# Attention, feed-forward and gMLP on one core: one-bank accumulators in phase two, and earlier buffers for group 0's sums

## The chip, the cores and the metric

The kernel runs on one core of a Trainium2 chip. Every product is made on TensorE (PE) and summed in PSUM, whose eight banks hold 128 x 512 f32 numbers each. VectorE (DVE), ScalarE (ACT) and GpSimd (POOL) take the sums out and prepare operands; SyncE (SP) issues the DMAs. The metric is the device time of one execution in microseconds (us).

## The reference

For 8 batches of 576 positions and a width of 512, three stages follow each other:

```python
out  = softmax(q_c @ k_c.T / 8) @ v_c           # 8 heads, chunks of 64 positions
x    = x + relu(LN(x) * g @ w_ch1) @ w_ch2      # 512 -> 2048 -> 512
h    = gelu_tanh(x @ w_in)                      # 512 -> 1024
u, v = h[..., :512], h[..., 512:]
v_s  = w_sg @ (LN(v) * g_ln) + b_sg             # over the 576 positions
out  = x + (u * v_s) @ w_out
```

The x of the second line is the attention's output, its heads side by side.

## The kernel before, in words

**Numbers.** A product of f32 matrices is made from fp16 halves: each operand is split into a rounded half ("hi") and the rest ("lo"), and three matmuls (hi·hi, hi·lo, lo·hi) are summed. Most large products also use seven products of quarter blocks in place of eight. Such a product needs sums and differences of quarters ahead of it (three instructions on DVE), a rounding to hi (ACT) and a subtraction for lo (DVE or POOL).

**Phase one.** The 8 x 576 positions are 36 tiles of 128, in 18 blocks of two. A block goes through attention, the layer norm, ff1 and ff2. For blocks 4 to 17 this is done in eight passes: `ff1p(b, j)` makes 24 matmuls (L639), ACT takes the result through relu (L654), DVE makes the sums (L661 to L663), ACT rounds (L666) and DVE or POOL subtracts (L668); `ff2p(b, j)` then makes 21 matmuls (L690), two passes later. After the last pass of a block DVE (L708), ACT (L713) and POOL (L718) put its x together, a DMA stores it in `x2d` in DRAM (L574), and DVE takes its largest magnitude (L201). In the middle of phase one the weights of phase two are split too, through buffers of the pool `stB`, which `close_st` closes when that is done.

**Group 0's x2 sums.** Phase two works on four groups of 9 tiles. For each group x is loaded again, as five panels p = 0 to 4 (`x2_make`): loads into `xs` (L900), sums on DVE (L907 to L909, panels 0 to 3), rounding on ACT into `hh` (L924), subtraction on DVE (L927), and two DMA transpositions, of the hi and of the lo half, into `x2T` (L922). For group 0 this is part of phase one's plan (`first_x2`). It has one `xs` and one `hh` buffer, allocated in the pool `x2L`, which `open_x2` opens where the attention's pool has been closed, thus after the attention of block 17. Its lo half goes into a buffer of the ring `xT`, which is the operand of ff1p.

**Phase two.** Each group makes v (L1206, L1231), u (L1248, L1269), the spatial product in two halves e = 0 and 1 (`s_units`: four units each, one 128 x 512 matmul L1301 and one 128 x 64 matmul L1302 per step; evacuated on DVE by L1312 and, for the 64-wide part, L1331; multiplied by u on POOL, L1319), the scale of the gated product (`red` by DVE, transposed on PE by L206), its halves, and nine `o_unit`s (product L1381, evacuated with the addition of x by L1389 on DVE). The outputs of v and u are taken out by ACT (L1113) and DVE (L1117).

**What sets the order.** The class `Plan` holds every operation with its engine, an assumed duration, a priority and the keys that it reads and writes. It plays the program through with the assumed durations and writes the instructions in the order that results; phase one is one plan, phase two another. Waits between instructions are put in by the framework, per tile: an instruction that writes a tile waits for the earlier readers of that tile.

**PSUM.** One pool, `psA`, is open throughout. It has two tiles of two banks, `pair0` and `pair1`, and four of one, `bank2`, `bank3`, `bank6` and `bank7`. Phase two takes accumulators from a ring `R` of eight one-bank pieces by `take`, so that four of the pieces are halves of a pair:

```python
R = [bank[2], bank[3], pair[1][:, 0], pair[1][:, 1], pair[0][:, 0], pair[0][:, 1], bank[6], bank[7]]
```

Of the kernel before, what the change touches and what calls it, by code (L numbers as in the profile page):

```python
# [9 lines left out]
F16 = mybir.dt.float16  # L10
F32 = mybir.dt.float32
# [121 lines left out]
def fused_kernel(ctx: ExitStack, tc, qkv, w1, w2, g1, w_in, w_out, wsgt, wsgs, g2, b_sg, out):  # L133
# [4 lines left out]
    small = ctx.enter_context(tc.tile_pool(name="small", bufs=1))  # L138
    dram = ctx.enter_context(tc.tile_pool(name="dram", bufs=1, space=bass.MemoryType.DRAM))
    psA = tc.tile_pool(name="psA", bufs=1, space=PSUM)  # L140
    ps = ctx.enter_context(psA)
    pair = [ps.tile([P, 2, 512], F32, name=f"pair{i}") for i in range(2)]
    bank = {i: ps.tile([P, 512], F32, name=f"bank{i}") for i in (2, 3, 6, 7)}
    x2d = [dram.tile([P, D], F32, name=f"x2d{t}") for t in range(NT)]
# [15 lines left out]
    def close_pool(key):  # L160
        pools.pop(key)[0].__exit__(None, None, None)
# [692 lines left out]

    def close_st():
        bW["stp"].__exit__(None, None, None)

    def open_x2():
        close_pool("att")
        p = ctx.enter_context(tc.tile_pool(name="x2L", bufs=1))  # L860
        x2p["T"] = p.tile([P, 2, 7, 2, D], F16, name="x2T")
        x2p["T8"] = p.tile([P, 2, 4, P], F16, name="x2T8")
        x2p["xs"] = [p.tile([P, 9, 256], F32, name="xs0")]
        x2p["hh"] = [p.tile([P, 7 * 256], F16, name="hh0")]

    def x2_cols(g0, n):

# [16 lines left out]
    def x2_make(pl, g, p, pr):  # L884


        o = pl.op
        xs, X = x2_buf(pl, "xs")
        hi, H = x2_buf(pl, "hh")
        if pl is plan:  # L890
            lo = x2p.get("lo") or palloc("xT", 2, [P, 2, 4, 256], F16, px)
            x2p["lo"], L = lo, lambda: lo.t.rearrange("p a k t -> p (a k t)")
        else:
            lo, L = x2_buf(pl, "hh")
        if p < 4:
            tiles, a, n = ((g * GT + p + 4, (0, 2)), (g * GT + p, (1, 3))), 1, 7
        else:
            tiles, a, n = ((g * GT + 8, (0, 1)),), 0, 2
        for t, c in tiles:
            o("SP", 730, lambda t=t, c=c: nc.sync.dma_start(  # L900
                out=X()[:, c[0]:c[1] + 1:c[1] - c[0]], in_=x2d[t].rearrange("p (n e) -> p n e", n=2)
            ), rd=["x2L"] + [f"x2d{t}"] * (pl is plan), wr=[xs], lat=2200, prio=pr)

        def sums():
            a = X()
            two = lambda x, y: a[:, x:y + 1:y - x]
            nc.vector.tensor_tensor(out=two(6, 8), in0=two(1, 3), in1=two(0, 2), op=ALU.subtract)  # L907
            nc.vector.tensor_tensor(out=two(4, 7), in0=two(0, 6), in1=two(2, 8), op=ALU.add)
            nc.vector.tensor_tensor(out=a[:, 5], in0=a[:, 2], in1=a[:, 6], op=ALU.subtract)  # L909

        if p < 4:
            o("DVE", 1800, sums, wr=[xs], prio=pr)
        src = lambda: X()[:, a:a + n].rearrange("p n e -> p (n e)")
        w = n * 256
        sc = i2g[:, g:g + 1]

        def turned(x, b, B):
            if p < 4:
                out, c = x2p["T"][:, x].rearrange("p n k t -> p (n k) t"), slice(p * 128, p * 128 + 128)
            else:  # L920
                out, c = x2p["T8"][:, x], slice(0, 128)
            nc.sync.dma_start_transpose(out=out[:, :, c], in_=B()[:, 0:w])  # L922

        o("ACT", 60 + w, lambda: nc.scalar.activation(out=H()[:, 0:w], in_=src(), func=AF.Copy, scale=sc),  # L924
          rd=[xs, f"sx{min(g, 1)}"], wr=[hi], prio=pr)

        o("DVE", 80 + w * 26 // 25, lambda: nc.vector.scalar_tensor_tensor(  # L927
            out=L()[:, 0:w], in0=src(), scalar=sc, in1=H()[:, 0:w], op0=ALU.mult, op1=ALU.subtract
        ), rd=[xs, f"sx{min(g, 1)}", hi], wr=[lo], prio=pr)

        def last():
            for x, b, B in ((0, hi, H), (1, lo, L)):
                o("SP", 1300 * n // 4, lambda x=x, b=b, B=B: turned(x, b, B), rd=[b], wr=[f"xT{x}{p}"], lat=2200, prio=pr)

        return last

    def first_x2():
        pr = 9500
        op("DVE", 100, lambda: absmax(redg[:, 0:1], x2mx[:, 0:GT]), rd=[f"x2mx{i}" for i in range(GT)], wr=["redg"], prio=pr)
        par(e2g[:, 0:1], redg[:, 0:1], ["redg"], ["x2e"], pr)  # L940
        op("DVE", 600, lambda: x2_cols(0, 1), rd=["win_s"], wr=["x2e", "sx0"], prio=pr)
        for p in range(5):
            x2_make(plan, 0, p, pr)()

    tops = [Buf(f"top{i}", None) for i in range(2)]
    with tc.manual_schedule():
# [76 lines left out]
        for b in range(B0, NB):  # L1023
# [7 lines left out]
            if b in (B0 + 1, B0 + 2, B0 + 3):  # L1031
                half[b - B0 - 1]()
            if b == B0 + 3:
                op(None, 0, close_st, rd=["wsg_s"] + done, wr=["Braw", "Btmp", "topB", "stC"], prio=0)
        for b, j in todo:
            ff2p(b, j)
        op(None, 0, open_x2, rd=["stC"], wr=["x2L"] + ATT, prio=0)
        first_x2()
        nff.append(0)

# [6 lines left out]
        plan.idle = busy  # L1047
        plan.run()

        close_pool("w2s")  # L1050
        pX.__exit__(None, None, None)
        wA.__exit__(None, None, None)
# [13 lines left out]

        plan2 = Plan()
        op2 = plan2.op
        R = [bank[2], bank[3], pair[1][:, 0], pair[1][:, 1], pair[0][:, 0], pair[0][:, 1], bank[6], bank[7]]
        turn_, seq = [0], [0]  # L1070
        xk = [f"xT{x}{p}" for x in range(2) for p in range(5)]
        op2(None, 0, lambda: None, wr=xk + ["x2L", "sx0", "ident"])

        def take(n):
            r = [(turn_[0] + k) % 8 for k in range(n)]
# [427 lines left out]
```

## Time and profile before

| | |
|---|---|
| median of 3 runs | 1282.22 us (1281.65 to 1283.42) |
| the profiled execution's own time | 1283.95 us |
| its span | 1282.2 us |
| TensorE busy | 1210.5 us, 94% |
| VectorE busy | 819.9 us, 64% |
| ScalarE busy | 558.8 us, 44% |
| GpSimd busy | 485.2 us, 38% |
| mean granted clock of TensorE | 0.991 |
| phase one's last product ends at | 865.8 us |

Times in rows are microseconds from the start of the span. Names of tiles stand without their numbers, so that `pair` is either of the two pairs, and `bank` any of the four single banks. A granted clock of 1 is 2.4 GHz, and 0.5 is 1.2 GHz. In a bracket behind a row stands the idle time of the engine before it, and what ended it.

### The profile page before, as it was taken

How to read it: one execution, taken by the hardware profiler on the slowest of the kernel's cores; microseconds unless marked ns; L12 is line 12 of the kernel's file. 1: busy time of each engine (PE TensorE's matmuls, PEld its weight loads, DVE VectorE, ACT ScalarE, POOL GpSimd, SP SyncE). 2: the span in 40 equal slices, each digit the busy share in tenths (PEclk: the TensorE clock that was granted, in tenths of full speed). 3: DMA queues.
4: the chain of work that ended last, by engine and by line, in shares of the span. 5: the costliest groups of instructions: out<-in, count | busy, mean ns of one | idle time of the engine just before them, and what ended most of it. 6: DMA issues, size and time to landing. Idle time of an engine off the chain costs nothing. (4 is left out here: it accounts for less than half of the span.)

```text
span 1282.2 us, 27034 instructions
## 1 busy us (share of the span) xinstructions
PE 1210.5 (94%) x11412; PEld 893.1 (70%) x11412; DVE 819.9 (64%) x1520; ACT 558.8 (44%) x844; POOL 485.2 (38%) x415
## 2 busy tenths in 40 slices
PE   7899999898998999999999999988899999999998
PEld 5687644677887888888888888866455556446453
DVE  6885135988677656665665565666778378457445
ACT  6776303455764533334333333333544444434320
POOL 3553203544585644434444334422432131232220
PEclk9999999999999999999999999999999999999999
DMA  9762002274222222122122201443353462362203
GB/s 319 242 210 80 1 33 75 75 208 127 83 59 59 59 67 67 51 67 65 55 64 57 69 26 50 92 99 91 85 129 107 86 153 91 86 121 66 82 1 115
DMA packets 140377, 117.81 MB, mean 92 GB/s; under 512 B 104928, under 2 KB 113120, under 8 KB 140256
## 3 DMA queue, kind: packets, MB, share of 16 engines
q1 hardware_dynamic: 140256, 116.09, 33.3%
q8 instruction: 89, 1.46, 0.5%
q14 instruction: 32, 0.26, 0.1%
HBM read 72.02 MB, written 18.87 MB: 71 GB/s over the span
## 5 line engine op out<-in xcount | busy, mean ns | idle before, releaser
L639 PE MATMUL bank<-xT,w1h 128*128 128x256 f16 x1792 | 304.1, 274 | 0.4 <-DVE x L568 0.4
L690 PEld LDWEIGHTS <-arena 128*128 128x128 f16 x2352 | 229.4, 99 | 44.5 <-issue 8.0
L639 PE MATMUL bank<-xT,w1l 128*128 128x256 f16 x896 | 245.6, 274 | 0.0
L668 POOL TENSOR_TENSOR arena<-arena 128x896 f16<-128x896 f32 x69 | 132.5, 1920 | 223.8 <-ACT arena L666 223.7
L639 PEld LDWEIGHTS <-w1h 128*128 128x128 f16 x1792 | 173.9, 98 | 23.5 <-issue 1.2
L666 ACT ACTIVATE arena<-arena 128x896 f16<-128x896 f32 x112 | 106.2, 949 | 186.4 <-DVE arena L663 102.2
L661 DVE TENSOR_TENSOR arena<-arena 128x256 f32<-128x256 f32 x112 | 76.2, 681 | 103.4 <-ACT arena L654 103.2
L690 PE MATMUL pair<-w,arena 128*128 128x256 f16 x672 | 112.3, 276 | 6.2 <-ACT arena L666 4.3
L690 PE MATMUL pair<-w2s,arena 128*128 128x256 f16 x672 | 111.5, 275 | 5.7 <-ACT u L713 5.2
L654 ACT ACTIVATE arena<-bank 128x512 f32<-128x512 f32 x112 | 66.4, 593 | 108.2 <-PE bank L639 108.2
L1319 POOL TENSOR_TENSOR uT<-uT,vs 128x512 f32<-128x512 f32 x30 | 47.1, 1571 | 135.9 <-DVE vs L1312 105.6
L639 PEld LDWEIGHTS <-w1l 128*128 128x128 f16 x896 | 88.2, 98 | 10.7
L690 PE MATMUL bank<-w,arena 128*128 128x256 f16 x672 | 93.2, 275 | 0.0
L535 PE MATMUL bank<-xT,w1h 128*128 128x256 f16 x512 | 86.9, 274 | 3.8 <-DMA xT<-hl 2.7
L718 POOL TENSOR_TENSOR x<-x,u 128x256 f32<-128x256 f32 (+1 forms) x60 | 65.2, 1116 | 45.9 <-DVE x L708 34.1
L1206 PEld LDWEIGHTS <-x2T 128*128 128x128 f16 x672 | 66.2, 99 | 17.7 <-issue 7.4
L1381 PE MATMUL pair<-wout,gh 128*128 128x512 f16 x208 | 61.9, 379 | 8.9 <-DVE xr L1389 7.0
L535 PE MATMUL bank<-xT,w1l 128*128 128x256 f16 x256 | 70.2, 274 | 0.0
L668 DVE TENSOR_TENSOR arena<-arena 128x896 f16<-128x896 f32 x43 | 57.5, 1337 | 19.7 <-ACT arena L666 19.7
L1301 PE MATMUL pair<-wsg,vh 128*128 128x512 f16 x190 | 60.1, 380 | 9.0 <-DVE vs L1312 8.1
L535 PEld LDWEIGHTS <-w1h 128*128 128x128 f16 x512 | 49.2, 98 | 15.1 <-issue 3.1
L662 DVE TENSOR_TENSOR arena<-arena 128x256 f32<-128x256 f32 x112 | 54.7, 488 | 3.8
(274 smaller groups left out, 2381.3 us busy)
## 6 DMA issues: line engine op xcount, KB each, us to landing
straw<-in_w SPq DMA_DIRECT2D x16, 1023.8 KB, 6.0
qkl<-in_qkv SPq DMA_DIRECT2D x26, 512.0 KB, 3.7
x2d<-x SPq DMA_DIRECT2D x36, 256.0 KB, 2.0
xs<-x2d SPq DMA_DIRECT2D x36, 256.0 KB, 3.3
xr<-x2d SPq DMA_DIRECT2D x36, 256.0 KB, 2.9
out<-xr SPq DMA_DIRECT2D x36, 256.0 KB, 2.5
vl<-in_qkv SPq DMA_DIRECT2D x26, 256.0 KB, 2.7
qk<-in_qkv SPq DMA_DIRECT2D x10, 512.0 KB, 6.1
```

Source lines behind the costliest of these rows:

```text
L535: nc.tensor.matmul(acc, lhsT=w[j][:, k, fc], rhs=xT.t[:, x, k], start=(n == 0), stop=(n == 11))
L639: nc.tensor.matmul(acc[:, y * 256:y * 256 + 256], lhsT=w[j][:, k, fc], rhs=xT.t[:, x, k], start=(n == 0), stop=(n == 11),)
L654: op("ACT", 600, lambda: nc.scalar.activation(out=o.t[:, 0:4].rearrange("p n t -> p (n t)"), in_=acc, func=AF.Relu, scale=0.5), rd=[kb] + ...
L661: nc.vector.tensor_tensor(out=two(6, 8), in0=two(1, 3), in1=two(0, 2), op=ALU.subtract)
L662: nc.vector.tensor_tensor(out=two(4, 7), in0=two(0, 6), in1=two(2, 8), op=ALU.add)
L666: op("ACT", 950, lambda: nc.scalar.activation(out=h.t[:, 0], in_=o.t[:, 1:8], func=AF.Copy), rd=[o] + ar, wr=[h], prio=-100)
L668: op(lo[0], lo[1], lambda: lo[2].tensor_tensor(out=h.t[:, 1], in0=o.t[:, 1:8], in1=h.t[:, 0], op=ALU.subtract), rd=[o], wr=[h], prio=-100)
L690: nc.tensor.matmul(acc, lhsT=h.t[:, x, n], rhs=r(y), start=(first and j == 0 and m == 0), stop=(j == 7 and m == 2), skip_group_check=True,)
L718: op("POOL", ns, lambda: nc.gpsimd.tensor_tensor(out=d(), in0=d(), in1=v(), op=ALU.add), rd=u + ["q6", "q5", "q7"], wr=[x], prio=-50)
L1206: nc.tensor.matmul(ap[:, q * 256:q * 256 + 256], lhsT=xT[:, x, a, k, c], rhs=right(b, 1, k, w), start=(first and n == 0), stop=(k == 1 and ...
L1301: nc.tensor.matmul(ap, lhsT=v[:, fc], rhs=w[:, 0:512], start=(n == 0), stop=end)
L1381: nc.tensor.matmul(ap, lhsT=x[:, k, c], rhs=w[:, k], start=(n == 0), stop=(n == 11))
```

## The change

It has two parts. First, `psA` is closed after phase one's plan, and a pool `psB` of eight tiles of one bank each, `pb0` to `pb7`, is opened. The ring `R` lists them in the order 4, 5, 2, 3, 0, 1, 6, 7, which are the same banks in the same places as before. Second, `xs0` and `hh0` are allocated in a new pool `xsL` in the room of `stB`, when `close_st` runs. The loads of group 0 now need that pool alone, and the transpositions need `x2L`. The hi half is transposed first; for panels 0 and 1 the lo half then overwrites `hh0`, and for panels 2 to 4 it goes into the `xT` buffer as before. Line numbers from L857 on are 3 to 9 higher after the change, and 9 higher in phase two: L907 to L909 are L910 to L912, L927 is L936, L1206 is L1215, L1301 is L1310, L1381 is L1390.

```diff
-    ps = ctx.enter_context(psA)
+    ps = psA.__enter__()
...
     def close_st():
         bW["stp"].__exit__(None, None, None)
+        p = ctx.enter_context(tc.tile_pool(name="xsL", bufs=1))
+        x2p["xs"] = [p.tile([P, 9, 256], F32, name="xs0")]
+        x2p["hh"] = [p.tile([P, 7 * 256], F16, name="hh0")]
...
     def open_x2():
...
-        x2p["xs"] = [p.tile([P, 9, 256], F32, name="xs0")]
-        x2p["hh"] = [p.tile([P, 7 * 256], F16, name="hh0")]
...
     def x2_make(pl, g, p, pr):
...
-        if pl is plan:
+        if pl is not plan:
+            lo, L = x2_buf(pl, "hh")
+        elif p < 2:
+            lo, L = hi, H
+        else:
             lo = x2p.get("lo") or palloc("xT", 2, [P, 2, 4, 256], F16, px)
             x2p["lo"], L = lo, lambda: lo.t.rearrange("p a k t -> p (a k t)")
-        else:
-            lo, L = x2_buf(pl, "hh")
...
-            ), rd=["x2L"] + [f"x2d{t}"] * (pl is plan), wr=[xs], lat=2200, prio=pr)
+            ), rd=["xsL"] + [f"x2d{t}"] * (pl is plan), wr=[xs], lat=2200, prio=pr)
...
+        def turns(*xs_):
+            for x, b, B in xs_:
+                o("SP", 1300 * n // 4, lambda x=x, b=b, B=B: turned(x, b, B), rd=["x2L", b], wr=[f"xT{x}{p}"], lat=2200, prio=pr)
+
+        if pl is plan:
+            turns((0, hi, H))
         o("DVE", 80 + w * 26 // 25, lambda: nc.vector.scalar_tensor_tensor(
             out=L()[:, 0:w], in0=src(), scalar=sc, in1=H()[:, 0:w], op0=ALU.mult, op1=ALU.subtract
-        ), rd=[xs, f"sx{min(g, 1)}", hi], wr=[lo], prio=pr)
+        ), rd=[xs, f"sx{min(g, 1)}"] + [hi] * (hi is not lo), wr=[lo], prio=pr)
+        if pl is plan:
+            return turns((1, lo, L))
+        return lambda: turns((0, hi, H), (1, lo, L))
...
         plan.run()
 
+        psA.__exit__(None, None, None)
+        psB = ctx.enter_context(tc.tile_pool(name="psB", bufs=1, space=PSUM))
+        bank = [psB.tile([P, 512], F32, name=f"pb{i}") for i in range(8)]
...
-        R = [bank[2], bank[3], pair[1][:, 0], pair[1][:, 1], pair[0][:, 0], pair[0][:, 1], bank[6], bank[7]]
+        R = [bank[k] for k in (4, 5, 2, 3, 0, 1, 6, 7)]
```

On TensorE, in group 0's spatial product, the start of the second half of a unit's matmuls. `pair1_64` and `pb3` are the same bank there, `vh` and `vl` the halves of v, `wsg` those of w_sg. Before:

```order
L1301 LDWEIGHTS vh_10698
L1301 MATMUL pair1_64<-wsg_3164,vh_10698 128x512 [waits DVE_49]
L1302 LDWEIGHTS vh_10698
L1302 MATMUL bank3_66<-wsg_3164,vh_10698 128x64
L1301 LDWEIGHTS vl_10699
```

The same rows after the change:

```order
L1310 LDWEIGHTS vh_10713
L1310 MATMUL pb3_10695<-wsg_3164,vh_10713 128x512
L1311 LDWEIGHTS vh_10713
L1311 MATMUL pb5_10697<-wsg_3164,vh_10713 128x64
L1310 LDWEIGHTS vl_10714
```

The wait for DVE is gone in this row; in all, 18 matmuls of L1301 and 17 of L1381 have a wait for another engine in the order before, and 11 and 7 after. No row of phase two has another place on any engine.

On TensorE, at the border of the phases: the last matmuls of phase one (`w2s7` and `arena` are the operands of its last ff2p pass) and the first of phase two. Before:

```order
L690 LDWEIGHTS arena_114
L690 MATMUL bank7_68<-w2s7_2552,arena_114 128x256
L1206 LDWEIGHTS x2T_9921 [waits DMAHW4_49,PE_49]
L1206 MATMUL bank2_65<-win_3162,x2T_9921 128x256
L1206 LDWEIGHTS x2T_9921
```

After:

```order
L690 LDWEIGHTS arena_114
L690 MATMUL bank7_68<-w2s7_2552,arena_114 128x256
L1215 LDWEIGHTS x2T_9932 [waits DVE_49,DMAHW4_49,PE_49]
L1215 MATMUL pb4_10696<-win_3162,x2T_9932 128x256 [waits Activation_49]
L1215 LDWEIGHTS x2T_9932
```

The first product now waits for DVE and ScalarE too: for the last L708 and the last L713, which read tiles of the old pool.

On DVE, at the end of phase one, the rows up to the last ff2 evacuation (L661 to L663 are an ff1p pass's sums, L668 its subtraction, `xs0` group 0's panel). Before, panel 3:

```order
L907 TENSOR_TENSOR xs0_9923<-xs0_9923 128x2x256 [waits DMAHW1_49,DMAHW0_49]
L908 TENSOR_TENSOR xs0_9923<-xs0_9923 128x2x256 [waits DVE_49]
L909 TENSOR_TENSOR xs0_9923<-xs0_9923 128x256
L927 SCALAR_TENSOR_TENSOR xT_10140<-xs0_9923,i2g_128,hh0_9924 128x1792 [waits DMAHW7_49,Activation_49]
L661 TENSOR_TENSOR arena_114<-arena_114 128x2x128 [waits Activation_49]
L662 TENSOR_TENSOR arena_114<-arena_114 128x2x128 [waits DVE_49]
L663 TENSOR_TENSOR arena_114<-arena_114 128x128
L668 TENSOR_TENSOR arena_114<-arena_114 128x896 [waits PE_49,Activation_49]
L708 SCALAR_TENSOR_TENSOR x_10651<-pair0_63,c_c2b_175,x_10651 128x256 [waits PE_49,Activation_49]
```

After, from panel 3's subtraction on:

```order
L936 SCALAR_TENSOR_TENSOR xT_10330<-xs0_5485,i2g_128,hh0_5486 128x1792 [waits DMAHW6_49,Activation_49]
L661 TENSOR_TENSOR arena_114<-arena_114 128x2x128 [waits Activation_49]
L662 TENSOR_TENSOR arena_114<-arena_114 128x2x128 [waits DVE_49]
L663 TENSOR_TENSOR arena_114<-arena_114 128x128
L668 TENSOR_TENSOR arena_114<-arena_114 128x896 [waits PE_49,Activation_49]
L661 TENSOR_TENSOR arena_114<-arena_114 128x2x128 [waits Activation_49]
L662 TENSOR_TENSOR arena_114<-arena_114 128x2x128 [waits DVE_49]
L663 TENSOR_TENSOR arena_114<-arena_114 128x128
L936 SCALAR_TENSOR_TENSOR xT_10330<-xs0_5485,i2g_128,hh0_5486 128x512 [waits DMAHW4_49,DMAHW3_49,Activation_49]
L661 TENSOR_TENSOR arena_114<-arena_114 128x2x128 [waits Activation_49]
L662 TENSOR_TENSOR arena_114<-arena_114 128x2x128 [waits DVE_49]
L663 TENSOR_TENSOR arena_114<-arena_114 128x128
```

Before, panel 3's sums and subtraction stand directly ahead of the last pass's sums, and panel 4's subtraction (128x512) behind the last L708; after, two other passes' sums stand between panel 3's subtraction and the last pass's, and panel 4's subtraction is ahead of the last pass's. Panel 0's sums stand where block 8 is worked on, some 400 DVE rows before its subtraction, and its two loads on SP ahead of a load of q and k. The subtractions of panels 0 and 1 have one wait, for a DMA (the transposition of `hh0`). On TensorE two small pieces of phase one have another place: a group of the attention's transpositions (L304) comes three matmuls later, and at the border of blocks 16 and 17 an ff2p pass that was split around half an ff1p pass is whole.

## Rows read from the trace of the kernel before

**Rows 1.** The page, part 1: busy us, share of the span, instructions.

```profile
PE 1210.5 (94%) x11412; PEld 893.1 (70%) x11412; DVE 819.9 (64%) x1520; ACT 558.8 (44%) x844; POOL 485.2 (38%) x415
```

**Rows 2.** TensorE's waits: line, what ended them: us in total, times, longest.

```profile
PE pair L1301 <- DVE vs L1312: 8.1, 9, 1.3
PE pair L1381 <- DVE xr L1389: 7.0, 8, 1.1
PE pair L690 <- ACT u L713: 5.6, 9, 1.2
PE pair L690 <- ACT arena L666: 4.3, 1, 4.3
...
PE pair L1381 <- DVE hv L1117: 1.9, 1, 1.9
...
PE pair L1301 <- DVE vt L1331: 0.9, 1, 0.9
...
PE pair L1302 <- DVE vs L1312: 0.8, 1, 0.8
```

**Rows 3.** Timeline from 1232 us: start, us, engine, line, operation [idle before, releaser].

```profile
1232.27 0.75 DVE L1312 SCALAR_TENSOR_TENSOR vs<-pair,c_c,bb 128x512 f32<-128x512 f32 x1 [4.46 <-PE pair L1301]
1233.08 0.38 PE L1301 MATMUL pair<-wsg,vh 128*128 128x512 f16 x1 [0.88 <-DVE vs L1312]
```

**Rows 4.** Windows: length, busy us of PE PEld DVE ACT POOL, PEclk, DMA share, GB/s.

```profile
755.00:799.00 44.00, 43.44 (x421) 38.12 (x419) 25.46 (x52) 16.01 (x24) 18.77 (x17) 1.00 0.14 37
859.60:866.50 6.90, 5.70 (x26) 3.52 (x27) 3.06 (x6) 1.62 (x4) 0.10 (x1) 0.51 0.40 84
880.00:885.00 5.00, 5.00 (x33) 3.77 (x32) 3.68 (x6) 0.63 (x1) 0.00 (x0) 0.66 0.09 32
925.00:1283.00 358.00, 333.69 (x2258) 184.56 (x2256) 211.87 (x374) 133.85 (x192) 90.09 (x75) 1.00 0.39 96
```

**Rows 5.** Timeline of phase one's last passes, 845 to 860 us, all engines.

```profile
845.78 0.49 PE L690 MATMUL pair<-w,arena 128*128 128x256 f16 x3
...
847.75 0.49 PE L690 MATMUL bank<-w2s,arena 128*128 128x256 f16 x3
...
853.69 1.79 ACT L924 ACTIVATE hh<-xs,i2g 128x1792 f16<-128x1792 f32 x1 [3.14 <-DVE xs L909]
...
855.52 2.08 DVE L927 SCALAR_TENSOR_TENSOR xT<-xs,i2g,hh 128x1792 f16<-128x1792 f32 x1 [1.86 <-ACT hh L924]
857.52 0.42 DVE L661 TENSOR_TENSOR arena<-arena 128x256 f32<-128x256 f32 x1
...
859.72 0.61 PE L690 MATMUL pair<-w,arena 128*128 128x256 f16 x2 [4.27 <-ACT arena L666]
```

**Rows 6.** Timeline of the border of the phases, 865 to 874 us.

```profile
864.96 0.84 PE L690 MATMUL bank<-w2s,arena 128*128 128x256 f16 x3
...
866.24 0.48 DVE L708 SCALAR_TENSOR_TENSOR x<-bank,c_c2a,x 128x256 f32<-128x256 f32 x1
...
873.14 0.69 ACT L1113 ACTIVATE o<-bank,e2g 128x512 f32<-128x512 f32 x1 [7.55 <-DMA x2d<-x]
...
873.88 0.38 PE L1206 MATMUL bank<-win,x2T 128*128 128x256 f16 x2 [2.43 <-ACT o L1113]
```

**Rows 7.** Timeline at group 3's last scale, 1257.7 us.

```profile
1257.74 0.16 DVE L201 TENSOR_REDUCE red<-gm 128x1 f32<-128x5 f32 x1
...
1258.29 0.27 PE L206 MATMUL pair<-ident,red 128*1 128x128 f32 x1
```

**Rows 8.** Tiles `xs`, then `x2T`, 750 to 900 us: ns minimum/median/maximum; DMA landing us.

```profile
L908 DVE TENSOR_TENSOR xs<-xs x6: 691/1474/2346, 797.8 to 882.0; 128x512 f32<-128x512 f32 x6
...
L927 DVE SCALAR_TENSOR_TENSOR xT<-xs,i2g,hh x5: 1043/2083/2165, 811.6 to 866.6; 128x1792 f16<-128x1792 f32 x4, 128x512 f16<-128x512 f32 x1
...
DMA to landing us min/median/max: 3.0/3.4/6.9
...
DMA to landing us min/median/max: 2.4/4.0/4.2
```

More of the change, by code (lines that the diff above doesn't have):

```diff
@@ L925, in x2_make @@
           rd=[xs, f"sx{min(g, 1)}"], wr=[hi], prio=pr)
+        def turns(*xs_):
[3 more added lines that the diff above has]
+            turns((0, hi, H))
         o("DVE", 80 + w * 26 // 25, lambda: nc.vector.scalar_tensor_tensor(
             out=L()[:, 0:w], in0=src(), scalar=sc, in1=H()[:, 0:w], op0=ALU.mult, op1=ALU.subtract
-        ), rd=[xs, f"sx{min(g, 1)}", hi], wr=[lo], prio=pr)
[L931 to L935, printed above, removed]
+        ), rd=[xs, f"sx{min(g, 1)}"] + [hi] * (hi is not lo), wr=[lo], prio=pr)
+        if pl is plan:
+            return turns((1, lo, L))
+        return lambda: turns((0, hi, H), (1, lo, L))
     def first_x2():
@@ L942, in first_x2 @@
         for p in range(5):
-            x2_make(plan, 0, p, pr)()
+            x2_make(plan, 0, p, pr)
     tops = [Buf(f"top{i}", None) for i in range(2)]
@@ L1033, in fused_kernel @@
             if b == B0 + 3:
-                op(None, 0, close_st, rd=["wsg_s"] + done, wr=["Braw", "Btmp", "topB", "stC"], prio=0)
+                op(None, 0, close_st, rd=["wsg_s"] + done, wr=["Braw", "Btmp", "topB", "xsL"], prio=0)
         for b, j in todo:
             ff2p(b, j)
-        op(None, 0, open_x2, rd=["stC"], wr=["x2L"] + ATT, prio=0)
+        op(None, 0, open_x2, rd=["xsL"], wr=["x2L"] + ATT, prio=0)
         first_x2()
@@ L1068, in fused_kernel @@
         op2 = plan2.op
-        R = [bank[2], bank[3], pair[1][:, 0], pair[1][:, 1], pair[0][:, 0], pair[0][:, 1], bank[6], bank[7]]
+        R = [bank[k] for k in (4, 5, 2, 3, 0, 1, 6, 7)]
         turn_, seq = [0], [0]
         xk = [f"xT{x}{p}" for x in range(2) for p in range(5)]
-        op2(None, 0, lambda: None, wr=xk + ["x2L", "sx0", "ident"])
+        op2(None, 0, lambda: None, wr=xk + ["xsL", "x2L", "sx0", "ident"])
         def take(n):
```

## The prediction, made before the changed kernel had run

> **What bounds the kernel now.** I began with the page's busy line. TensorE works 1210.5 of 1282.2 us [rows 1]: 71.7 us are all that a change without fewer products can win, and a microsecond is won only where TensorE stands still. So the second view is the waits of TensorE, sorted by what ended them [rows 2]. Five of its lines belong to phase two and name as releaser an evacuation on DVE that read a tile called `pair`: 8.1 + 7.0 + 1.9 + 0.9 + 0.8 = 18.7 us in 20 waits. The timeline shows one of them close up [rows 3]: DVE's L1312 reads an accumulator from 1232.27 for 0.75 us, and the next L1301 product begins at 1233.08, after 0.88 us of standing still. Both are called `pair`, but they are different halves: the ring hands out one bank at a time, and the reader has the bank of the unit before. The first two pieces of the order say the same: the product waits for DVE in the kernel before and for nothing after the change, while the rest of the order stays. The wait is for the tile's name and not for the bank.
>
> Third, the windows [rows 4]. In 755 to 799 TensorE is busy 43.44 of 44.00 us: within phase one's regular blocks there is 0.56 us to win and no more. From 925 to 1283 it is idle 358.00 - 333.69 = 24.3 us, of which the 18.7 are most, at a granted clock of 1.00, so none of the difference there can come from the clock. Between the two lies a bad place: 859.6 to 866.5 has a granted clock of 0.51, the lower of the two levels (1.2 GHz), after 4.27 us in which TensorE had nothing.
>
> The timeline of that place [rows 5] tells why. ScalarE's rounding of panel 3 (L924) runs 853.69 to 855.48, VectorE's subtraction of it (L927) 855.52 to 857.60, and only behind it stand the sums of phase one's last ff1 pass (L661 at 857.52), whose halves the last ff2p product (L690, 859.72) needs. TensorE stopped at 859.72 - 4.27 = 855.45. Its last ff2p product ends at 864.96 + 0.84 = 865.80 [rows 6]: 10.35 us for a pass that takes, at the full clock, from 845.78 to 847.75 + 0.49 = 848.24, that is 2.46 us [rows 5].
>
> **The change part by part.** *One-bank tiles.* No instruction is added: TensorE's queue has as many rows as before and in phase two the same order. Of L1301's products with a wait in the order 18 become 11, of L1381's 17 become 7. Removed are the 20 waits of the five lines, 18.7 us [rows 2]. What is late next is the true wait behind each: the L206 transposition waits for the reduction `red`, a unit's product for its own bank's last reader, eight banks back. I let all gains stand except one, since DVE, which gives the banks back, works only 211.87 of the 358.00 us [rows 4] and has done with the older banks. The exception is the kernel's end: `red` is ready at 1257.74 + 0.16 = 1257.90 and L206 runs at 1258.29 [rows 7], 0.39 us of slack, while one removed wait just ahead is 0.84 us. About 0.5 us of it comes back as a wait for `red`. Phase two: 18.7 - 0.5 = **18.2 us**. Bounds: 18.7 if nothing comes back; half, 9.1, if the next true waits stand closer than the trace says.
>
> *The border of the phases.* The new pool opens when the old one is closed, so the first product of phase two, which waited for transposed data alone, now also waits for the last readers of the old banks (third piece of the order): the last L713 copy on ScalarE and the last L708 on DVE, which ends at 866.24 + 0.48 = 866.72 against 865.80 for the last product [rows 6]. That is about 1 us. Queued behind it on TensorE are the rest of the first unit's products, and they run into a wait of 2.43 us at 873.88 for L1113, which itself had waited 7.55 us for the store of x and not for TensorE [rows 6]. The 2.43 us cover it: **0**. Without the cover, 1 us.
>
> *The early panels.* Buffers in room that is free from mid phase one let panel 0's two loads and its sums (L907 to L909) go to about block 8 of phase one. VectorE is busy 25.46 of 44.00 us in a regular window [rows 4], so three sums of 1 to 5 us find room; cost 0. On SP the two loads wait for GpSimd's last subtraction on the weights, whose room they take, and behind them stands one load of q and k for a later block; 0, with one load's 3.4 us [rows 8] as the upper bound. What this moves at the end is what counts: each panel's VectorE work comes one place earlier, so that the sums and the subtraction of panel 3 stand two passes higher and only the 512-column subtraction of panel 4 stands ahead of the last pass's sums (the DVE pieces of the order). The 4.27-us stop and the slow clock that follows lose their cause. If the last pass were fed without any stop, 10.35 - 2.46 = 7.9 us would be won.
>
> Against that stand: panel 4's subtraction, in the before behind phase one, at 1.04 us [rows 8], now ahead of the last sums, of which I count 0.8 since the sums wait for ScalarE in any case; one wait for ScalarE's copies out of the bank (L713 holds L690 up 5.6 us in 9 waits, 0.62 each [rows 2]), which the last pass keeps, 0.6; a second like it at the border of blocks 16 and 17, where the order now runs a whole ff2p pass in one piece (0.6). 7.9 - 0.8 - 0.6 - 0.6 = **5.9 us**. Upper bound 7.9; lower bound, stop unchanged and the additions paid: -1.7, rounded with the 0.2 by which an evacuation slips.
>
> *Panels 0 and 1 subtract in place.* The subtraction overwrites the rounded half, so it now waits until that has been transposed: a new wait on VectorE, and behind it in the queue stand the sums of an ff1 pass, for which ScalarE, then TensorE wait. A transposition takes 2.4 to 4.2 us from issue to landing, median 4.0 [rows 8]. VectorE does other work between panel 0's rounding and its subtraction (in the order, some 400 instructions), and one pass lies between them for panel 1; I take 0, since TensorE had 0.56 us of idle in 44 with two passes of products queued ahead [rows 4]. Upper bound: the exposed 3.4 + 4.0 of one load and one transposition (rival three).
>
> The moved sums may meet GpSimd. L908 takes 691 ns at least, 1474 in the middle and 2346 at most [rows 8], and the long ones lie beside GpSimd's L668. Two of the moved sums lengthened by 2.35 - 0.69 = 1.66 us would leave 5.9 - 3.3 = 2.6 us of the tail. I keep 5.9, because the sums that gate the tail's last pass are no longer these.
>
> The Trainium skill, SBUF — State Buffer, section "Who interferes with whom", has VectorE and GpSimd share a pair of ports that one holds exclusively. By that rule each moved sum beside GpSimd's subtraction pays the longer time, and the whole gain would be 18.2 + 2.6 = 20.8 us; the spread of L908 in the trace agrees with it.
>
> Sum: 18.2 + 5.9 = 24.1 us. The profiled execution took 1283.95 us, 1.73 above the median 1282.22: 1259.9 for it, and **1258.1 us** for the median.
>
> **The rivals.**
> *One: the tail gives nothing.* VectorE and ScalarE still collide with the last passes, the last pass is fed late by some other step, and the clock falls as before. For it: the whole panel work still ends within phase one. Against: the order puts panel 3 clear of the last pass. 1282.2 - 18.2 = 1264.0.
>
> *Two: the true waits stand close.* Half of phase two's 18.2 us returns as waits for a bank's own reader or for `red`; TensorE runs ahead and ScalarE and GpSimd don't follow. For it: what gives a bank back is still a chain through DVE, ACT and GpSimd. Against: in 925 to 1283 DVE is busy 211.87, ACT 133.85, POOL 90.09 of 358 us [rows 4], so none is near the bound. 1282.2 - 9.1 - 5.9 = 1267.2.
>
> *Three, the other side: VectorE held by the panels.* A panel's load, 3.4 us at the median [rows 8], and for the in-place ones a transposition, 4.0, stand open in front of VectorE's queue, which then holds the sums of ff1 passes while TensorE empties its queue. Panel 0 exposes 4.0, panel 1 3.4 + 4.0, panels 2 to 4 3.4 each: 21.6 us, and no gain in the tail: 1264.0 + 21.6 = 1285.6. It turns the sign once more than 18.2 us are exposed. For it: the order shows a wait for a DMA at each of these instructions. Against: panel 0 is loaded and rounded far ahead, the panels wait for their loads in the kernel before too, and of L690's waits for the passes only one, 4.3, is longer than a fraction of a microsecond [rows 2].
>
> *Four, slower: single banks and the clock.* Products that go through eight separate banks stop briefly at each change of bank, and the clock falls. A fall as in 880 to 885 has a mean granted clock of 0.66 [rows 4], so (1 - 0.66) x 5 = 1.7 us lost. At the 20 places of the removed waits that is 34 us: 1258.1 + 34 = 1292. It turns the sign from 24.1 / 1.7 = 14 falls on. Against: 1.00 in 925 to 1283 [rows 4], with the same ring of eight banks and 20 stops more.
>
> The Trainium skill, TensorE: Matmul & The Clock Gate, section "A second HAM failure mode: psum-queue depth-cycling", tells of a kernel whose clock oscillated while it cycled through banks. By that rule the time would be rival four's; the trace does not agree so far, by the 1.00 just named.
>
> *Five: nothing.* The waits only change their names, because the banks are the same: 1282.2.
>
> **How the numbers follow.** Forecast 0.75, one 0.15, two 0.06, three 0.02, four 0.01, five 0.01. The range takes in the forecast's own bounds: with all of 18.7 + 7.9 = 26.6 us it would be 1255.6, and an execution's scatter of 1.1 us takes it to 1254.5; with the tail at -1.7 it is 1282.2 - 18.2 + 1.7 = 1265.7, rounded up to 1266, which covers rival one. Left out are two to five, 0.10, and the forecast's edges. A difference of 0.2%, 2.6 us, is about what a measurement of this kernel can tell from no change: only three and four are slower by more (0.03), five lies within (0.01), the rest is faster (0.96).
>
> **What would show it.** In the profile after: no line of TensorE's waits that names L1310 or L1390 with a DVE reader of another bank, and idle time of about 6 us from the 925-us place to the end in place of 24.3; the last ff2p pass in about 4 to 5 us in place of 10.35, at a granted clock near 1; the 2.4-us wait at the border shorter or equal. I am wrong if the waits reappear under `red` or a bank's own reader, if TensorE's idle time grows in the regular windows of phase one (panels 0 and 1), or if the granted clock falls between units.

## The result, and the profile after

The changed kernel takes 1252.67 us (median of 4 runs, 1251.7 to 1254.36) where the kernel before takes 1282.82 us beside it (1281.65 to 1284.96): a ratio of 0.9765, 95% interval 0.9747 to 0.9782. That is 30.2 us less; 24.1 had been forecast, and the median lies 1.8 us below the range. The direction and both places of the gain were right, the size of phase two's term was not.

The profiled execution has a span of 1249.9 us. Its page has the same number of matmuls as [rows 1], and a smaller busy time:

```profile
PE 1202.5 (96%) x11412; PEld 890.9 (71%) x11412; DVE 816.2 (65%) x1520; ACT 559.4 (45%) x844; POOL 481.7 (39%) x415
```

8.0 us of TensorE's busy time have gone although not one product has. Keep that in mind for what follows: busy time is the time that at least one row covers. Rows of matmuls that follow each other at once overlap, so that with a stop between them they cover more; and rows are longer at the lower clock.

TensorE's waits from 881 us to the last product, where [rows 2] has five lines of `pair`, are these (the view leaves out stops under 0.15 us):

```profile
PE pb L1257 <- DVE uT L1126: 1.5, 2, 1.0
PE pb L1215 <- DVE vt L1340: 0.8, 1, 0.8
```

And from 790 to 881 us, where [rows 2] has the stop of 4.3 us:

```profile
PE pb L1215 <- DVE hv L1126: 2.5, 1, 2.5
PE pb L1215 <- DVE x L708: 2.0, 1, 2.0
PE pair L690 <- DVE arena L668: 1.5, 1, 1.5
PE pair L690 <- ACT x L713: 1.1, 2, 0.6
```

To see where the time went I took the start of the same product, counted in program order, in both traces, and subtracted. All tables below are made so; a stage is named by where it lies in the kernel before.

| us gained against the first profile of before | 0 to 326 | 326 to 803 | 803 to 855 | 855 to 889 | 889 to 1278 | all |
|---|---|---|---|---|---|---|
| the change | 1.8 | 0.0 | -2.4 | 8.9 | 23.9 | 32.3 |
| the change, second profile | -3.1 | 0.0 | -1.9 | 8.4 | 24.0 | 27.4 |
| the kernel before, second profile | 0.6 | 0.0 | 0.0 | 0.3 | 0.1 | 1.0 |

The first 326 us scatter by some microseconds from one execution to the next; behind them the two profiles of a kernel agree, stage by stage, to half a microsecond. So the change is worth 8.9 - 2.4 = 6.5 us at the end of phase one and 24 us in phase two: 30.5, near the 30.2 of the medians.

The second profiles are runs of their own, with these expectations.

> The changed kernel once more, for what differs from one execution to the next. Theory: the 1.8 us that the first 330 us of the changed kernel's profile gained, and the low clock at 880 us of the kernel before, are scatter: they move by a microsecond or two here; the waits of phase two are the same to 0.1 us. Rival: the moved L304 transpositions won the 1.8 us: they are there again.

> The kernel before once more, one look. Theory: the waits of phase two are deterministic: from the first v unit's end (889 us in the first profile) to the last product it takes 388.6 us again, within 0.1 us, with 23.0 us of idle time in 26 stops; the first 330 us move by a microsecond or two. Rival: phase two scatters by microseconds too, and the 24 us found there are partly scatter.

The changed kernel took 1253.88 us (4 runs, ratio 0.977, 0.9745 to 0.9795), the kernel before 1282.93 in its one run. The same L639 product, the first behind the same L690 group, starts at 326.01 in the first profile of before; in the two profiles of the changed kernel it is one of these:

```profile
324.19 0.38 PE L639 MATMUL bank<-xT,w1h 128*128 128x256 f16 x2
```

```profile
329.09 0.38 PE L639 MATMUL bank<-xT,w1h 128*128 128x256 f16 x2
```

One is 1.8 us early, the other 3.1 us late, so the moved L304 transpositions (the rival) won nothing that stands out of the scatter. The other half of the theory, that the low clock at 880 us is scatter, fell: the second profile of before has a granted clock of 0.87 in 877 to 890 too, and neither profile of the changed kernel has a low stretch there. From 889 us on the kernel before took 388.55 us where it had taken 388.63, with the same 26 stops, so the rival there, scatter in phase two, is refuted.

### The profile page after: what moved, and what is told of

It is laid out like the page before. It is cut to its first block, busy times and chain, and to the rows that moved or that the text cites. A ratio compares the mean times of both kernels' runs of the same rounds, so it can differ in the third digit from the quotient of the medians.

```text
span 1249.9 us, 27025 instructions
## 1 busy us (share of the span) xinstructions
PE 1202.5 (96%) x11412; PEld 890.9 (71%) x11412; DVE 816.2 (65%) x1520; ACT 559.4 (45%) x844; POOL 481.7 (39%) x415
## 4 chain that ended last, share of the span: by engine, by line
PE 70%; DVE 14%; DMA 5%; ACT 4%; POOL 3%; issue 3%; SPq 0%; ACTq 0%; DVEq 0%; POOLq 0%
PE bank L639 16%; PE pair L690 9%; PE pb L1390 7%; PE pb L1310 7%; PE bank L690 6%; PE pb L1215 5%; PE bank L535 5%; PE pb L1257 5%; PE pair L556 3%; PE bank L556 2%; DVE arena L661 1%; DVE tf L599 1%; DMA xs<-x2d 1%; PE pair L294 1%; DMA straw<-in_w 1%
## 5 line engine op out<-in xcount | busy, mean ns | idle before, releaser
L639 PE MATMUL bank<-xT,w1h 128*128 128x256 f16 x1792 | 302.9, 274 | 0.4 <-DVE x L568 0.4
L690 PEld LDWEIGHTS <-arena 128*128 128x128 f16 x2352 | 228.3, 98 | 40.9 <-issue 9.4
L639 PE MATMUL bank<-xT,w1l 128*128 128x256 f16 x896 | 245.0, 273 | 0.0
L668 POOL TENSOR_TENSOR arena<-arena 128x896 f16<-128x896 f32 x69 | 132.7, 1924 | 224.4 <-ACT arena L666 224.3
L639 PEld LDWEIGHTS <-w1h 128*128 128x128 f16 x1792 | 173.6, 98 | 23.3 <-issue 1.3
L661 DVE TENSOR_TENSOR arena<-arena 128x256 f32<-128x256 f32 x112 | 76.8, 686 | 102.3 <-ACT arena L654 102.2
L690 PE MATMUL pair<-w2s,arena 128*128 128x256 f16 x672 | 110.6, 274 | 7.0 <-ACT u L713 5.9
L690 PE MATMUL pair<-w,arena 128*128 128x256 f16 x672 | 111.2, 274 | 2.9 <-DVE arena L668 1.5
L639 PEld LDWEIGHTS <-w1l 128*128 128x128 f16 x896 | 88.0, 98 | 10.4
L690 PE MATMUL bank<-w,arena 128*128 128x256 f16 x672 | 92.4, 274 | 0.0
L1328 POOL TENSOR_TENSOR uT<-uT,vs 128x512 f32<-128x512 f32 x30 | 40.7, 1357 | 132.6 <-DVE vs L1321 123.5
L1310 PE MATMUL pb<-wsg,vh 128*128 128x512 f16 x288 | 88.5, 380 | 0.0
L1390 PE MATMUL pb<-wout,gh 128*128 128x512 f16 x288 | 85.7, 379 | 0.0
L718 POOL TENSOR_TENSOR x<-x,u 128x256 f32<-128x256 f32 (+1 forms) x60 | 65.2, 1116 | 46.5 <-DVE x L708 34.1
L1215 PEld LDWEIGHTS <-x2T 128*128 128x128 f16 x672 | 66.0, 99 | 16.5 <-issue 6.6
L668 DVE TENSOR_TENSOR arena<-arena 128x896 f16<-128x896 f32 x43 | 57.3, 1333 | 17.9 <-ACT arena L666 17.8
```

Of the source, the lines that this page charges most:

```text
L639: nc.tensor.matmul(acc[:, y * 256:y * 256 + 256], lhsT=w[j][:, k, fc], rhs=xT.t[:, x, k], start=(n == 0), stop=(n == 11),)
L668: op(lo[0], lo[1], lambda: lo[2].tensor_tensor(out=h.t[:, 1], in0=o.t[:, 1:8], in1=h.t[:, 0], op=ALU.subtract), rd=[o], wr=[h], prio=-100)
L690: nc.tensor.matmul(acc, lhsT=h.t[:, x, n], rhs=r(y), start=(first and j == 0 and m == 0), stop=(j == 7 and m == 2), skip_group_check=True,)
L718: op("POOL", ns, lambda: nc.gpsimd.tensor_tensor(out=d(), in0=d(), in1=v(), op=ALU.add), rd=u + ["q6", "q5", "q7"], wr=[x], prio=-50)
L1215: nc.tensor.matmul(ap[:, q * 256:q * 256 + 256], lhsT=xT[:, x, a, k, c], rhs=right(b, 1, k, w), start=(first and n == 0), stop=(k == 1 and ...
L1310: nc.tensor.matmul(ap, lhsT=v[:, fc], rhs=w[:, 0:512], start=(n == 0), stop=end)
```

## The experiments

**One part at a time.** First the tiles without the buffers:

```diff
+        psA.__exit__(None, None, None)
+        psB = ctx.enter_context(tc.tile_pool(name="psB", bufs=1, space=PSUM))
+        bank = [psB.tile([P, 512], F32, name=f"pb{i}") for i in range(8)]
...
-        R = [bank[2], bank[3], pair[1][:, 0], pair[1][:, 1], pair[0][:, 0], pair[0][:, 1], bank[6], bank[7]]
+        R = [bank[k] for k in (4, 5, 2, 3, 0, 1, 6, 7)]
```

> The eight one-bank tiles alone; group 0's buffers stay as before. Theory A: a stall of TensorE costs its idle time and about 0.17 us of refilling, since a 512-column matmul is shown with 0.38 us and its neighbours start 0.21 us apart, and the name-only waits of the first v and u units count too: 24 us less than before, 1259, and 1256.5 if the low clock at 880 us goes too. Rival B: a stall costs only the idle time that the trace shows: 18.2 us less, 1264.6. In both the stop of 4.3 us ahead of phase one's last ff2p pass stays.

Measured: 1258.59 us, ratio 0.9805 (0.9781 to 0.9829). That is theory A's 1259, and 6 us under rival B's price. (Line numbers of phase two are 6 lower here than in the changed kernel, 3 lower in the next run and 1 higher in the one behind it.) Then the buffers without the tiles (from the changed kernel, the three lines and the ring taken back):

```diff
-        psA.__exit__(None, None, None)
-        psB = ctx.enter_context(tc.tile_pool(name="psB", bufs=1, space=PSUM))
...
-        R = [bank[k] for k in (4, 5, 2, 3, 0, 1, 6, 7)]
+        R = [bank[2], bank[3], pair[1][:, 0], pair[1][:, 1], pair[0][:, 0], pair[0][:, 1], bank[6], bank[7]]
```

> The early buffers alone; phase two keeps the pairs. Theory A: the last ff2p pass wins 6.5 us, the border of blocks 16 and 17 loses 2.4: 4.1 us less than before, 1278.7; 1276.4 if the low clock at 880 us came from the stop in phase one's tail. Rival: phase two's start waits for the store of x and not for TensorE, so that the tail's gain is eaten there: 1282. If the two parts add up, the gains of this run and of the banks alone make 30 us.

Measured: 1277.68 us, ratio 0.995 (0.9933 to 0.9967). Against 1283.4 for the kernel before in the same session the two parts win 24.8 and 5.7 us, together 30.5, and the changed kernel 29.5; from the product at 326 us on the profiles have 25.3 and 5.6 for the parts and 30.4 and 30.5 for the whole. So they add up to within the scatter, and the rival, by which the tail's gain is eaten at phase two's start, is refuted.

**The wait for a name, more of it.** The eight accumulators as halves of four tiles:

```diff
-        bank = [psB.tile([P, 512], F32, name=f"pb{i}") for i in range(8)]
+        two = [psB.tile([P, 2, 512], F32, name=f"pb{i}") for i in range(4)]
+        bank = [two[i // 2][:, i % 2] for i in range(8)]
```

> The changed kernel with its eight accumulators as halves of four two-bank tiles: the wait by name at every ring place, and not at four of eight. In the order the spatial product's and the output product's waiting matmuls are 45 (changed kernel 21, before 37). Theory A: each added wait costs about 1.05 us, of which 0.17 is no idle time in the trace: 24 waits, 25 us over the changed kernel, 1278, and TensorE's idle time in phase two rises by 0.17 us a wait less than the time. Rival B: rise of the time and of the idle time are the same. Rival C: the number of names costs nothing, only the stores' and the tail's order mattered: 1253.

Measured: 1297.48 us, ratio 1.0105 (1.0073 to 1.0138), 44 us above the changed kernel in the same session and slower than the kernel before. My count of the added waits, 24, was wrong, since I counted from the order of the spatial and the output product alone, and the waits of u, of v and of the scales change too: it is 40. The price of 1.05 us was nearly right, as the windows show. They run from the same product to phase two's last. The kernel before, then the changed one, then the four pairs (columns as in [rows 4]):

```profile
889.34:1277.97 388.63, 365.68 (x2468) 201.65 (x2467) 240.00 (x418) 159.33 (x224) 103.35 (x87) 1.00 0.37 92
```

```profile
881.03:1245.71 364.68, 362.31 (x2469) 201.29 (x2467) 239.87 (x417) 159.35 (x224) 99.73 (x87) 1.00 0.40 98
```

```profile
882.92:1290.80 407.88, 368.83 (x2468) 201.84 (x2467) 235.85 (x416) 158.64 (x224) 102.66 (x86) 1.00 0.34 88
```

TensorE's idle time is the length less its busy time: 22.95, 2.37 and 39.05 us. The busy time of the same matmuls is not the same: it grows with the stops of 0.1 us and more inside the stretch, 26 in the first, 4 in the second and 44 in the third. (365.68 - 362.31) / 22 = 0.153 and (368.83 - 362.31) / 40 = 0.163 us for each further stop. The reason stands in the rows themselves: a 512-column matmul is 0.38 us long in its row, in [rows 3] as here. Without a stop, the changed kernel's rows overlap:

```profile
1199.88 0.38 PE L1310 MATMUL pb<-wsg,vh 128*128 128x512 f16 x1
...
1200.10 0.19 PE L1311 MATMUL pb<-wsg,vh 128*128 128x64 f16 x1
```

The next one starts 0.22 us later, 0.16 before the first has ended. With a stop behind it this overlap is lost, and the busy time holds it as well. So a stop costs its idle time plus 0.16 us, in all 43.2 / 40 = 1.08 us here. The waits of the four pairs, in the same stretch and with the stop at its first product, are led by the one that the change removed (L1311 here is L1310 of the changed kernel):

```profile
PE pb L1311 <- DVE vs L1322: 12.5, 13, 1.8
PE pb L1391 <- DVE xr L1399: 8.7, 10, 1.1
PE pb L1391 <- DVE hv L1127: 3.7, 3, 2.0
PE pb L1258 <- DVE uT L1127: 3.4, 5, 1.1
```

**What moves the panels.** The room from mid phase one kept, but the lo halves of panels 0 and 1 put into the ring again:

```diff
-        elif p < 2:
+        elif p < 0:
```

> The changed kernel, but the lo halves of panels 0 and 1 go into the x operand's ring as in the kernel before; room from mid phase one and one-bank tiles stay. VectorE's order at the end of phase one is then that of before, since the ring's buffer is free only after block 16's last ff1 pass. Theory: the early room alone moves nothing, the subtraction in place does: the stop ahead of the last ff2p pass is back, the waits at the border of blocks 16 and 17 are gone, and the time is that of the one-bank tiles alone, 1258.6 (changed kernel 1253.3). Rival: the early loads and sums make the tail's gain: 1253.3.

Measured: 1255.89 us, ratio 0.9803 (0.9779 to 0.9827), by the medians between the tiles alone and the changed kernel, by the ratio not apart from the tiles alone (0.9805). Its waits from 790 to 886 us tell more than its time:

```profile
PE pair L690 <- ACT arena L666: 3.6, 1, 3.6
PE pb L1215 <- DVE hv L1126: 2.5, 1, 2.5
PE pb L1215 <- DVE x L708: 1.1, 1, 1.1
PE pair L690 <- DVE arena L668: 0.7, 1, 0.7
PE pair L690 <- ACT x L713: 0.6, 1, 0.6
```

The stop ahead of the last pass is back, and the 1.5-us wait at the border of blocks 16 and 17 is gone, both as the theory has it (the 0.7 us left for L668 stand in the last pass): without the subtraction in place the room alone does not let the panels go ahead. The subtraction in place without the room was not run. The theory's time, that of the tiles alone, was too long by the medians, and the profiles have 1.4 us between the two from 326 us on. The low clock behind the stop is much the same in both, 0.63 with the tiles alone and 0.60 here in 857 to 865 us, 0.82 and 0.84 in 865 to 877; but the second low stretch, which the tiles alone have at 880 us, does not come here. The tiles alone, then this kernel, both in 877 to 887 us:

```profile
877.00:887.00 10.00, 8.78 (x66) 7.22 (x66) 8.59 (x18) 2.26 (x3) 1.28 (x4) 0.83 0.26 90
```

```profile
877.00:887.00 10.00, 9.46 (x87) 8.49 (x87) 8.87 (x20) 3.89 (x6) 1.79 (x4) 1.00 0.18 70
```

Then in place for more panels, for all five and for three:

```diff
-        elif p < 2:
+        elif p < 6:
```

> The changed kernel with all five panels subtracting in place, so that each subtraction waits for the transposition of its hi half. In the order panel 2's subtraction stands two passes later, panel 3's directly ahead of the last pass's sums, panel 4's behind phase one. Theory: the wait of 1.5 us at the border of blocks 16 and 17 goes, the stop ahead of the last pass comes back with 3 to 5 us: 1255 to 1257. Rival, the prediction's third: VectorE is held for 4.0 us by each of the three new waits: 1265.

> The changed kernel with panel 2 in place too (panels 3 and 4 in the ring). Panel 2's subtraction then stands behind the first two passes' subtractions of block 17, and not ahead of them. Theory: the 1.5-us wait for VectorE's L668 at the border of blocks 16 and 17 goes, and nothing takes its place: 1251.7. Rival: panels 3 and 4 slip with it, and the last pass is fed a microsecond or two late: 1253 to 1255.

All five: 1255.86 us, ratio 0.980 (0.9777 to 0.9822), the time that the theory gave, though with smaller stops than it had (1.4 and 0.7 us ahead of and in the last passes, for 3 to 5) and one that it had not, 1.6 us for ScalarE's evacuation at phase two's start; the prediction's third rival, by which VectorE is held 4.0 us by each wait for a transposition, is off by 9 us. Three (`p < 3`): 1256.69 us, ratio 0.9793 (0.977 to 0.9817): a miss. The wait for L668 at the border did go, but panels 3 and 4 slipped, and the last ff2p passes now stop for 0.7 us three times and 0.6 once. By the medians two is the best of the tried numbers; the intervals of none, two, three and five overlap, but from the product at 326 us on two panels win 30.4 and 30.5 us, three and five 28.1 each, none 26.7.

**A better version.** The changed kernel still stops 2.5 us at 873 us, for an evacuation of v (`hv`) that stands in VectorE's queue behind the sums of group 1's first panels, and these wait for their loads:

```profile
870.70 0.69 DVE L910 TENSOR_TENSOR xs<-xs 128x512 f32<-128x512 f32 x1 [1.59 <-DMA xs<-x2d]
...
872.38 0.74 DVE L1126 SCALAR_TENSOR_TENSOR hv<-pb,e2g,hv 128x512 f32<-128x512 f32 x1
...
873.17 1.47 PE L1215 MATMUL pb<-winT,x2T 128*128 128x256 f16 x12 [2.53 <-DVE hv L1126]
```

The planner puts the sums there because it assumes that a load lands after 2.2 us. I gave it other landings for these panels:

```diff
-            ), rd=["xsL"] + [f"x2d{t}"] * (pl is plan), wr=[xs], lat=2200, prio=pr)
+            ), rd=["xsL"] + [f"x2d{t}"] * (pl is plan), wr=[xs], lat=4000 if g == 1 and p < 2 else 2200, prio=pr)
```

> The changed kernel with a longer assumed landing (6.0 for 2.2 us) for group 1's first two panels, so that their sums stand behind two more evacuations of group 0's v on VectorE. Theory: TensorE's wait of 2.5 us for hv at 873 us comes from the sums that wait for their loads ahead of hv; it goes: 1251. Rival: phase two's start then waits for the next evacuation, or the low clock lasts longer: 1253.3.

> The changed kernel with an assumed landing of 8.0 us for group 1's panel 0 alone, so that its sums stand behind the first unit's evacuations of v and the rest of the order moves in 50 rows of TensorE and 24 of VectorE. The version with both panels won 2.6 us by 889 us and lost 2.0 of it in group 1 to four waits of its own. Theory: the 2.5-us wait at 873 us goes and the later groups keep the changed kernel's waits: 2 us less, 1251 beside 1253.3. Rival: panel 1's sums now hold hv in panel 0's place: 1253.3.

> The changed kernel with an assumed landing of 4.0 us for group 1's first two panels: two evacuations of v come ahead of the first sums, 104 rows of TensorE and 34 of VectorE move. Theory: as for panel 0 alone, 1251, if hv no longer stands behind a load. Rival: the later order loses it again, as with 6.0 us: 1253.

Both panels at 6.0 us: 1252.85 us, ratio 0.9772 (0.9751 to 0.9793), a miss; panel 0 alone at 8.0 us: 1253.42 us, 0.9769 (0.9751 to 0.9788), another; both at 4.0 us: 1248.82 us, 0.9735 (0.9716 to 0.9755). The stages:

| us gained, as above | 803 to 855 | 855 to 889 | 889 to 1278 |
|---|---|---|---|
| the change (first, second profile) | -2.4, -1.9 | 8.9, 8.4 | 23.9, 24.0 |
| both panels, 6.0 us | -1.9 | 11.5 | 22.0 |
| panel 0, 8.0 us | -2.0 | 9.5 | 25.1 |
| both panels, 4.0 us | -2.0 | 11.5 | 25.2 |

The first wins 2.6 to 3 us at the start, where the stop for hv gives way to one of 1.1 us for ScalarE's evacuation and the clock does not fall either, and loses 2 in group 1, where its longer landing moved more of the order. The second moves the stop to the next evacuation (1.8 us at 884). The third has the gain of both, with the same stop for ScalarE (1.2 us) at the start. From the product at 326 us to the end it is 4.2 us ahead of the changed kernel, and the medians differ by 3.9 and 5.1; the intervals of the two ratios (0.9716 to 0.9755, 0.9747 to 0.9782) still touch. In its timeline the evacuations stand ahead of the sums:

```profile
870.20 0.75 DVE L1126 SCALAR_TENSOR_TENSOR hv<-pb,e2g,hv 128x512 f32<-128x512 f32 x1
871.46 1.47 PE L1215 MATMUL pb<-winT,x2T 128*128 128x256 f16 x12
871.72 0.69 DVE L910 TENSOR_TENSOR xs<-xs 128x512 f32<-128x512 f32 x1 [0.77 <-DMA xs<-x2d]
```

## Why the prediction was right in direction and wrong in size

**The step that failed** is the sum of phase two, "18.7 - 0.5 = 18.2 us". It measured 24.0 us, and 24.4 for the tiles alone. Three things were mis-sized in it.
- *The price of a stop.* I took the idle time that the waits view shows. Each stop costs 0.16 us beyond it, which the profile counts as busy time: 365.68 - 362.31 = 3.4 us for the 22 stops. This is the larger half of the 5.8 us by which the sum was short.
- *The count.* I took the five lines that name a product of the spatial or the output stage, and let those of L1248 and L1206 stand as true waits. In the same stretch before, they are

```profile
PE pair L1248 <- DVE uT L1117: 2.0, 3, 0.8
...
PE bank L1248 <- DVE uT L1117: 1.4, 1, 1.4
...
PE bank L1206 <- DVE vt L1331: 0.6, 1, 0.6
PE pair L1248 <- DVE o L1117: 0.3, 1, 0.3
```

  4.24 us before rounding, in six stops. At the same products 1.5 us are left, the two stops for `uT`: 2.7 us more than I had counted. Three of the six, on halves of a pair, are gone outright (0.26, 0.84 and 0.34 us), and the four pairs have all three again, so these were waits by name. The two on `bank` went from 1.41 to 0.56 us and from 0.60 to 0; a `bank` is a tile of one bank, so they were none, and why they shrank is not shown.
- *The give-back.* I had 0.5 us coming back at L206 of the kernel's end. None stands there, but two stops are new at about 1040 us: 0.76 us of L1215 for `vt`, the wait for a bank's own reader, and 0.10 us of L206 for `red`, too short for the view. That is 0.86 us, of the kind that I had named and at another place.

Idle time fell by 22.95 - 2.37 = 20.6 us, which is 18.7 + 2.7 - 0.86, and busy time by 3.4: 24.0.

**The rest, step by step.**
- *That the wait is for the tile's name* was right, and shown from both sides: one-bank tiles take all 20 stops of the five lines away, four pairs bring 40.
- *The true waits stand far enough behind* (against rival two): right. 4 stops are left from 881 us on, 2.4 us together: the three of the view and the 0.10 us.
- *The border of the phases at 0*: right. The new wait for L708 is there, 1.95 us where I had put about 1, and it is covered. From the last pass's first product to the one behind the stop for hv it is 873.17 - 855.82 = 17.35 us in the changed kernel, whose rows these are,

```profile
855.82 0.49 PE L690 MATMUL pair<-w,arena 128*128 128x256 f16 x3
...
857.53 0.49 PE L690 MATMUL pair<-w2s,arena 128*128 128x256 f16 x3 [0.56 <-ACT x L713]
...
858.51 0.49 PE L690 MATMUL bank<-w2s,arena 128*128 128x256 f16 x3
...
860.96 1.50 PE L1215 MATMUL pb<-win,x2T 128*128 128x256 f16 x12 [1.95 <-DVE x L708]
```

  and 875.68 - 858.39 = 17.29 us with the buffers alone, which have no such wait and stop 3.29 us for ScalarE's evacuation in its place:

```profile
858.39 0.49 PE L690 MATMUL pair<-w,arena 128*128 128x256 f16 x3
...
870.11 1.47 PE L1212 MATMUL bank<-win,x2T 128*128 128x256 f16 x12 [3.29 <-ACT o L1119]
...
875.68 0.59 PE L1212 MATMUL pair<-winT,x2T 128*128 128x256 f16 x2 [2.47 <-DVE hv L1123]
```

- *The tail at 5.9*: 6.5 us, and that it came so near is luck. The last pass takes 3.2 us (855.82 to 858.51 + 0.49) where it took 10.35 [rows 5, 6], without panel 4's subtraction holding it; I had left 0.8 us for that. But the border of blocks 16 and 17 costs 1.9 to 2.4 us where I had 0.6: the 0.56-us wait for L713 came as forecast, and with it one of 1.48 us (0.96 in the second profile) that I had not seen:

```profile
825.82 4.97 POOL L718 TENSOR_TENSOR x<-x 128x256 f32<-128x256 f32 x4
...
827.66 2.54 DVE L936 SCALAR_TENSOR_TENSOR xT<-xs,i2g,hh 128x1792 f16<-128x1792 f32 x1
...
830.13 1.61 DVE L668 TENSOR_TENSOR arena<-arena 128x896 f16<-128x896 f32 x1
...
831.80 0.28 PE L690 MATMUL pair<-w,arena 128*128 128x256 f16 x1 [1.48 <-DVE arena L668]
...
834.83 1.08 DVE L668 TENSOR_TENSOR arena<-arena 128x896 f16<-128x896 f32 x1
```

  Panel 2's subtraction stands ahead of a pass's L668, whose result the next product needs, and both are longer than where GpSimd does nothing beside them (2.08 us for a panel's subtraction in [rows 5], 1.08 for the next L668): GpSimd adds x here, L718, for 4.97 us. The place at which the moved work lands was thus the wrong one in my sum: I had looked for the collision with GpSimd in the sums at the end. The Trainium skill, SBUF — State Buffer, section "Who interferes with whom", tells of a lock between VectorE and GpSimd, and these rows agree; no run here moved GpSimd's additions, so the 1.48 us are not shown to come from it alone.

  Up to the product behind the stop for hv the stage of 855 to 889 us wins 6.9 us (6.4 in the second profile), with the border's loss 4.5 in either. The other 2.0 us come behind that stop: from there to the 889-us place it takes 7.86 us in both profiles of the changed kernel, at a granted clock of 1.00, and 9.85 in both of the kernel before, which has 0.66 in 880 to 885 us [rows 4]. 0.3 us of the 2.0 are a short stop at 889 us that is gone, the rest, 1.7, is what rival four puts on one such fall of the clock. My sum had no term for this. (Its lower bound of -1.7 does not come out of its terms either: 0.8 + 0.6 + 0.6 is 2.0.)
- *Panels 0 and 1 in place at 0*: right. VectorE does wait for panel 0's transposition,

```profile
794.10 3.17 DVE L936 SCALAR_TENSOR_TENSOR hh<-xs,i2g,hh 128x1792 f16<-128x1792 f32 x1 [1.74 <-DMA x2T<-hh]
```

  but nothing in 326 to 803 us moved on TensorE (0.0), and it has no stop from 803 to 821 us either, where panel 1's subtraction stands (812.84). Rival three is refuted by the run with all five in place.
- *Rival four, the clock*: refuted. The granted clock is 1.00 in phase two with eight banks and with 4, 26 or 44 stops. The rule of the Trainium skill that I had weighed there, TensorE: Matmul & The Clock Gate, section "A second HAM failure mode: psum-queue depth-cycling", does not show in this kernel.

## What to carry to other kernels

Waits are kept per tile: an accumulator that is handed out in pieces should be a tile for each piece, also where the pieces are the same banks. When stops are priced from a trace, add to the idle time the overlap that the next instruction loses (here 0.16 us beside a mean of 0.9), and list all of an engine's waits on a suspected tile, not those of the products that one thinks of first. Work that goes earlier also lands somewhere: look there for what is queued behind it.

## What the runs showed of the hardware that I had not expected

The clock falls near phase two's start in all but two of the kernels, but not at the same time. The kernel before, the tiles alone, the buffers alone and three or five panels in place have a low stretch at about 880 us (0.83 in 877 to 887 for the tiles alone, above). The changed kernel has it ahead of its stop for hv, and none behind it:

```profile
861.00:873.00 12.00, 9.64 (x72) 7.87 (x73) 5.32 (x9) 2.66 (x3) 3.49 (x5) 0.86 0.60 173
873.00:882.00 9.00, 8.83 (x81) 7.91 (x81) 8.41 (x19) 3.25 (x5) 1.79 (x4) 1.00 0.17 64
```

There it costs less, since TensorE runs into the 2.5-us stop anyway. In the stage from 855 to 889 the tiles alone win 0.9 us and the buffers alone 7.1, the two together 8.9 and 8.4: 0.3 to 0.8 us of the changed kernel's gain come only with both, hardly more than this stage scatters (0.3 and 0.5 us between two profiles of a kernel). With both panels at 4.0 us, and at 6.0, all three windows from 857 to 887 us are at 1.00; of the kernels profiled, these two stop least at that place. What the fall waits for was not settled: no run changed TensorE's idle time there by itself.
